# An attention and squared-ReLU kernel: its opening in a new load order, with most expanded weights spread by DMA, s applied at the eviction and the first attention put first

## The chip, the cores and the metric

The kernel runs on one core of one Trainium2 chip. The metric is the device time of a launch in microseconds (us). Engines: PE (TensorE), DVE (VectorE), ACT (ScalarE), POOL (GpSimd) and SP (SyncE), which here issues nearly all DMAs, in order.

## What is computed

```python
# x: (4, 12480, 128), inducing I: (32, 128), w_in: (128, 2048), w_out: (2048, 128); s, b: one number each
def mab(q, kv):
    a = softmax(q @ kv.T / sqrt(128))
    return a @ kv
h = mab(I, x)                     # 32 points for each of 4 batches
y = mab(x, h).reshape(49920, 128)
out = (s * relu(y @ w_in)**2 + b) @ w_out
```

## The kernel before

A block is 480 tokens (BLK), a tile two blocks (SB = 2); a batch has 13 tiles and 26 blocks. The last product is folded: y = A h, so y @ w_in is A times the small matrix h @ w_in. That matrix, 32 rows for a batch, is kept in `wst` as 128 rows: the rounded values twice and what rounding leaves twice ("expanded weights"). For each block the attention weights A, transposed and split in the same way, stand in a tile `a2t`. The steady work is 832 pairs (`pair(k)`, 8 pairs of 128 hidden columns x 2 in each of 104 blocks): two matmuls `wst` x `a2t` into `h` (L1002), a ReLU `r` (ACT or DVE), a rounded square (ACT, L1080), h times r (DVE, L1045), the difference to the rounded square (POOL or DVE, L1056), and six matmuls with `w_lo` and `w_hi` into the output bank (L1112). A block's output is evicted with a bias (L1125, L1127) and stored.

Which instruction comes when on each engine is decided at build time. `Plan` holds units of work (generators that yield an engine, a duration in us and events they wait for), gives each an urgency and always takes the one that its own clock has ready first, corrected by WEIGHT times urgency. `OPENING` is the set of constants for the first 16 pairs, the 26 sets of `STEADY` those for stretches of 32 pairs. Instructions stand in that order on each engine; on the chip semaphores enforce what depends on what.

The opening, in the order of its work:

- `opening()` issues the loads on SP. The tiles of batch 0 come in the order of `FIRST_GROUPS`; after the first the three small loads (inducing points `ind`, s, b) are issued, and after the places in `W_AFTER` one block of 512 columns of `w_in` or `w_out`. x tiles lie in five `xt` buffers, those in `X_HOME` in the buffers `gm` and `hm` of the later pairs.
- w_in and w_out come as 64-bit floats. `narrow` makes each block a 32-bit one with two maskings, two ACT steps, two DVE steps and a product on POOL or DVE; `split_w_out` multiplies a w_out block by s and splits it into `w_hi` (ACT, L455) and `w_lo` (DVE, L457).
- For each group `first_scores` makes the scores of the points, their exponentials and, with the tile not transposed, the values. The tile not transposed is made by `turn_x` (PE transposes L542, a copy for each half tile), or for those in `BY_DMA` loaded a second time as `xF` by `load_first`.
- When all maxima are there, `h_both` and `h_out` put the groups together and give `hT`, the 32 points.
- `w_unit` (four times) makes `wst` from `hT` and w_in: matmul L703, copy L705, subtraction L707. The later batches do it with `w_tiles` and `w_spread`: a matmul into 32 rows for each 512 columns, a copy and a subtraction into `whl`, and 16 DMA copies of 32 partitions into `wst`.
- `attend_first` makes `a2t` of block 0 alone, in a short form (L903 to L942). Then `front_work(0)` starts `attend(0, 0)` for blocks 1 to 3 (matmuls L853, a chain on DVE, copies L956 by DMA) and the bias. `keep_warm` puts matmuls on zeros into PE's gaps.

Of the kernel before, what the change touches and what calls it, by code (L numbers as in the profile page):

```python
# [56 lines left out]
W_IN_U = -100  # L57
W_OUT_U = -206.48
W_URGENCY = [12.71, 20.0, 50.1, 22.0]
W_LATE = -22.96  # L60
W_LEAN = {"Pool": -1.49}
FRONT_0 = -9.51
# [23 lines left out]
class Rules:  # L86
# [76 lines left out]
class Plan:  # L163
# [83 lines left out]
def tile_attn_relu2(ctx: ExitStack, tc: tile.TileContext, xT, xN, xF, indT, w_in, w_out, s_rep, b_rep, outT):  # L247
# [105 lines left out]
    def blocks_in(g):  # L353
        return min(GR, NBLK - g * GR)


    xt_tiles, xn_tiles = {}, {}
    raws = {}
    dma = [2.7]

    def landing(us):

        dma[0] = max(dma[0], plan.end + 3.0) + us
        if dma[0] < 5.0:
            dma[0], us = 6.2, dma[0]
            return us
# [962 lines left out]
```

## Time and profile before

| | |
|---|---|
| median of 3 runs | 1519.55 us (1518.22 to 1521.71) |
| the profiled execution: time / span | 1518.01 / 1516.2 us |
| busy: PE, DVE, ACT, POOL | 1495.3, 1435.3, 1465.4, 1443.7 us |
| granted TensorE clock, mean | 0.999 |
| first matmul of the first pair | 53.02 us |
| last matmul issued / last output DMA issued | near 1510.4 / 1511.96 us |

The span is from the first to the last thing that the profiler saw; the time of the execution is 1.8 us longer. A row gives the start or the window, then the busy time. PE's busy time overlaps from one matmul to the next, so that matmuls are better counted by their starts.

### The profile page before, as it was taken

What the parts mean: (1) busy time and instruction counts of PE and PEld (TensorE: products, weight loads), DVE (VectorE), ACT (ScalarE), POOL (GpSimd) and SP (SyncE); (2) the same over time, 40 slices, a digit from 0 to 9 for tenths busy, and PEclk for the clock granted to TensorE, in tenths of its full rate; (3) what the DMA queues carried; (4) which work ended last, traced back from release to release, by engine and by line L of the source; (5) the groups of instructions that cost most, each with busy time, mean ns of one, the idle gap of its engine ahead of it and who ended that gap; (6) DMA issues with size and microseconds to landing.
All of it is one profiled execution on the core that took longest, in us unless ns stands there. A gap on an engine that the chain in (4) does not pass through costs nothing.

```text
span 1516.2 us, 25236 instructions
## 1 busy us (share of the span) xinstructions
PE 1495.3 (99%) x8215; PEld 1294.9 (85%) x8215; DVE 1435.3 (95%) x1587; ACT 1465.4 (97%) x1767; POOL 1443.7 (95%) x725
## 2 busy tenths in 40 slices
PE   7899999999999999999999999999999999999998
PEld 5588888888888888888898888888889888888887
DVE  5899999999999999999999999999999999999998
ACT  6899999999999999999999999999999999999997
POOL 2599999999999999999999999999999999999998
PEclk9999999999999999999999999999999999999999
DMA  9244545534454454453455534544533334234332
GB/s 342 65 124 128 140 104 158 143 76 125 104 150 127 114 149 105 135 142 83 127 133 137 144 104 118 163 112 105 120 102 93 79 91 112 56 85 108 91 72 53
DMA packets 73810, 178.91 MB, mean 118 GB/s; under 512 B 13520, under 2 KB 40144, under 8 KB 73680
## 3 DMA queue, kind: packets, MB, share of 16 engines
q1 hardware_dynamic: 59280, 128.51, 27.2%
q0 software_dynamic: 14256, 48.67, 17.3%
q8 instruction: 67, 1.10, 0.3%
q14 instruction: 63, 0.52, 0.1%
q10 hardware_dynamic: 144, 0.12, 0.0%
HBM read 74.56 MB, written 25.56 MB: 66 GB/s over the span
## 4 chain that ended last, share of the span: by engine, by line
PE 69%; ACT 4%; issue 3%; POOL 3%; DVE 2%; DVEq 0%; ACTq 0%; POOLq 0%
PE x L1112 48%; PE h L1002 17%; POOL g L1056 3%; ACT r L1014 2%; ACT g L1080 2%; PE x L853 1%; DVE g L1045 1%; PE x L802 1%; PE x L762 1%; DVE h L1045 0%; DVE r L1016 0%; DVE gm L1027 0%; PE x L717 0%; ACT ob L1125 0%; POOL hm L1032 0%
## 5 line engine op out<-in xcount | busy, mean ns | idle before, releaser
L1056 POOL TENSOR_TENSOR g<-g,g 128x960 fp32r<-128x960 f32 x611 | 1399.2, 2665 | 21.7 <-DVE g L1045 13.4
L1112 PE MATMUL x<-g,w_hi 128*128 128x480 f32 x2932 | 920.1, 367 | 1.5 <-POOL g L1056 1.0
L1080 ACT ACTIVATE g<-r 128x960 fp32r<-128x960 f32 x733 | 713.4, 1008 | 12.0 <-PE x L1112 0.9
L1045 DVE SCALAR_TENSOR_TENSOR g<-h,r 128x960 f32<-128x960 f32 x611 | 688.5, 1146 | 24.2 <-ACT r L1014 13.7
L1014 ACT ACTIVATE r<-h 128x960 f32<-128x960 f32 x648 | 608.6, 970 | 12.5 <-PE h L1002 10.2
L1112 PEld LDWEIGHTS x<-g,w_hi 128*128 128x128 f32 x2932 | 550.8, 189 | 52.5 <-issue 6.3
L1112 PE MATMUL x<-g,w_lo 128*128 128x480 f32 x1466 | 537.4, 367 | 1.4 <-ACT g L1080 1.1
L1002 PE MATMUL h<-a2t,wst 128*128 128x480 f32 x1664 | 485.4, 374 | 3.7 <-DVE g L1045 3.2
L1002 PEld LDWEIGHTS h<-a2t,wst 128*128 128x128 f32 x1664 | 299.2, 189 | 82.2 <-issue 33.1
L1112 PEld LDWEIGHTS x<-g,w_lo 128*128 128x128 f32 x1466 | 277.0, 189 | 24.5 <-issue 2.6
L1016 DVE TENSOR_SCALAR r<-h 128x960 f32<-128x960 f32 x184 | 210.8, 1148 | 5.0 <-PE h L1002 3.8
L1056 DVE TENSOR_TENSOR g<-h,g 128x960 fp32r<-128x960 f32 x122 | 140.7, 1153 | 7.8 <-ACT g L1080 1.2
L1045 DVE SCALAR_TENSOR_TENSOR h<-h,r 128x960 f32<-128x960 f32 x122 | 141.0, 1155 | 0.9 <-ACT r L1014 0.8
L1027 DVE SCALAR_TENSOR_TENSOR gm<-h,r 128x960 f32<-128x960 f32 x99 | 113.3, 1145 | 4.3 <-ACT r L1014 4.1
L1032 POOL DMA_DIRECT2D hm<-gm x99 | 113.7, 1148 | 0.1
L1080 ACT ACTIVATE hm<-r 128x960 fp32r<-128x960 f32 x99 | 99.7, 1007 | 0.7
L1112 PE MATMUL x<-hm,w_lo 128*128 128x480 f32 x198 | 72.8, 368 | 0.0
L1112 PE MATMUL x<-hm,w_hi 128*128 128x480 f32 x198 | 72.5, 366 | 0.0
L1125 ACT ACTIVATE ob<-x,bias 128x480 f32<-128x480 f32 x101 | 66.8, 661 | 1.1 <-PE x L1112 0.5
L1112 PE MATMUL x<-hm,w_neg 128*128 128x480 f32 x198 | 56.3, 366 | 0.0
L1112 PEld LDWEIGHTS x<-hm,w_lo 128*128 128x128 f32 x198 | 37.4, 189 | 3.5 <-DVE hl L891 0.8
L1112 PEld LDWEIGHTS x<-hm,w_neg 128*128 128x128 f32 x198 | 37.4, 189 | 2.7
(152 smaller groups left out, 559.4 us busy)
## 6 DMA issues: line engine op xcount, KB each, us to landing
hm<-gm POOLq DMA_DIRECT2D x99, 480.0 KB, 5.3
xt<-in_xT_dram SPq DMA_DIRECT2D x96, 480.0 KB, 5.2
a2t<-hl SPq DMA_DIRECT2D x412, 60.0 KB, 2.0
out_dram<-ob SPq DMA_DIRECT2D x103, 240.0 KB, 2.1
xn<-in_xN_dram SPq DMA_DIRECT2D x18, 512.0 KB, 4.3
xn<-in_xN_dram SPq DMA_DIRECT2D x18, 448.0 KB, 4.8
wst<-whl SPq DMA_DIRECT2D x48, 64.0 KB, 2.0
g<-in_w_in_dram SPq DMA_DIRECT2D x4, 512.0 KB, 10.3
```

Of the source, the lines that this page charges most:

```text
L762: nc.tensor.matmul(ps[M * q:M * (q + 1), 0:BLK], ind_sb, xt[:, q % SB], start=True, stop=True)
L802: nc.tensor.matmul(ps[M * c:M * (c + 1), 0:P], eT[0:rows, n], xn_tiles[b, g, half][0][0:rows, n - half * TH], start=n < P // M, stop=n + P ...
L1002: nc.tensor.matmul(h[:, u, 0:BLK], wst[:, n * P:(n + 1) * P], by_turns(A), start=True, stop=True)
L1014: nc.scalar.activation(out=r, in_=hv, func=AF.Relu)
L1016: nc.vector.tensor_scalar(out=r, in0=hv, scalar1=0.0, scalar2=None, op0=ALU.max)
L1027: nc.vector.scalar_tensor_tensor(out=gm, in0=hv, scalar=-1.0, in1=r, op0=ALU.mult, op1=ALU.mult)
L1032: nc.gpsimd.dma_start(out=hi["t"].bitcast(F32).rearrange("p u t -> p (u t)"), in_=gm.rearrange("p u t -> p (u t)"), accum_op=ALU.add,)
L1045: nc.vector.scalar_tensor_tensor(out=g, in0=hv, scalar=0.0, in1=r, op0=ALU.max, op1=ALU.mult)
L1056: eng.tensor_tensor(out=g2, in0=g, in1=hi["t"].bitcast(F32), op=ALU.subtract)
L1080: nc.scalar.activation(out=hi["t"], in_=r, func=AF.Square)
L1112: nc.tensor.matmul(o, w, by_turns(g), start=first and n == 0, stop=left == 0 and n == len(ops) - 1)
L1125: nc.scalar.activation(out=ob, in_=o, func=AF.Identity, bias=bias, scale=1.0)
```

## The change

All of it is in the opening, except the eviction of each block, the last eviction, and the constants of `STEADY`.

- The loads follow a written list `ORDER`; i0 to i3 and o0 to o3 are blocks of w_in and w_out, f4 is the tile 4 loaded as `xF`. Four tiles come that way instead of two, into `g1` buffers instead of `xn`. `X_HOME` has three entries instead of six. The scores now wait for `ind`, which is ninth in the list.
- `FIRST_GROUPS` pairs other tiles; each weight block has an urgency of its own (`W_U`).
- `split_w_out` no longer multiplies by s: `w_hi` is a copy, `w_lo` a subtraction on DVE or POOL. The eviction multiplies by s instead.
- For batch 0 only the first 512 columns of `wst` come from `w_unit`; the other three quarters come from `w_tiles` and `w_spread`.
- `front_work(0)` waits until the second pair's matmuls are placed. `hold` keeps engines free for some time during `attend_first`.
- The last block is evicted in one piece by ACT and stored from ACT's queue.
- The planner's picture of the opening changes (engines begin at 0.7 to 2.3 us, PE takes twice as long before 8 us, an issue on SP takes 0.46 us), all constants of `OPENING` change, WEIGHT among them (0.0229 to 0.0032), and so do constants in most sets of `STEADY`.

```diff
-FIRST_GROUPS = ((2, 3), (4, 5), (6, 7), (8, 9), (10, 11), (12, 1), (0,))
-BY_DMA = [5, 9]
-W_AFTER = [1, 2, 6, 8, 1, 5, 7, 12]
-X_HOME = {3: "gm", 4: "hm", 5: "gm", 6: "hm", 8: "gm", 9: "hm"}
-FIRST_LEAN = {"ACT": -0.41}
+W_U = {"i0": 1513.8106, "i1": 2422.085, "i2": -276.0022, "i3": -391.7822, "o0": -749.0613, "o1": -185.0209, "o2": -164.7013, "o3": -106.3167}
+W_URGENCY = [-200.2675, 255.7455]
+FIRST_U = {"h": -16.5052, "sums": 121.8764, "attend": -87.9451}
+HOLD = [0.1554, 1.3641, 0, 0]
+W_LEAN = {"Pool": -1.9541}
+FIRST_GROUPS = ((2, 3), (4, 6), (5, 7), (8, 9), (12, 11), (10, 1), (0,))
+ORDER = [
+    "x2", "i0", "x3", "s", "x6", "x7", "x5", "i2", "ind", "f4", "x4", "i1", "x8", "x9", "x12",
+    "f11", "x11", "x10", "f9", "i3", "x1", "o0", "x0", "o1", "o3", "f1", "b", "o2",
+]
+ISSUE = 0.46
+BEGIN = {"SP": 0.74, "PE": 1.8, "ACT": 2.0, "DVE": 2.3, "Pool": 2.2}
+COLD = 8.0
+FIRST_LAND = 2.05
+X_HOME = {5: "hm", 6: "gm", 9: "hm"}
+FIRST_LEAN = {"ACT": -0.5563}
-OPENING = Rules(0.0229, 0.0865, -0.624, 0.022, ...)
+OPENING = Rules(0.0032, 0.1938, -0.1311, 0.0328, ...)
 STEADY = [
...
     def split_w_out(c):
...
-        nc.scalar.mul(w_hi[:, sl, :], raw[:, sl, :], s_sb)
-        yield "DVE", 0.63, LOCK
-        nc.vector.scalar_tensor_tensor(
-            out=w_lo[:, sl, :], in0=raw[:, sl, :], scalar=s_sb, in1=w_hi[:, sl, :].bitcast(F32),
-            op0=ALU.mult, op1=ALU.subtract,
+        nc.scalar.copy(out=w_hi[:, sl, :], in_=raw[:, sl, :])
+        yield dict(DVE=0.63, Pool=1.5), W_LEAN, LOCK
+        (nc.gpsimd if plan.eng == "Pool" else nc.vector).tensor_tensor(
+            out=w_lo[:, sl, :], in0=raw[:, sl, :], in1=w_hi[:, sl, :].bitcast(F32), op=ALU.subtract
         )
...
     def load_first(j):
-        n, free = ring_in_order("xn", 2)
+        yield "SP", ISSUE, room("g1", G1)
...
     def first_scores(g, ps, *waits):
...
-        yield "PE", 0.45 * len(js), *[("x", 0, j, 1) for j in js], *waits
+        yield "PE", 0.45 * len(js), "ind", *[("x", 0, j, 1) for j in js], *waits
...
     def w_tiles(b, ps, *waits):
-        yield "PE", 1.19, ("hT", b), *[("w_in", c) for c in range(F // WC)], *waits
+        yield "PE", 1.19, ("hT", b), *[("w_in", c) for c in range(F // WC)], *([] if b else [("wst", 0, 0)]), *waits
...
-        for c in range(F // WC):
+        for c in range(0 if b else 1, F // WC):
             plan.spawn(w_spread(b, c, whl, wst), SPREAD, plan.end + LAT)
...
     def attend_first():
...
+        hold(DVE=HOLD[0], Pool=HOLD[1])
...
         plan.set("first")
+        yield "SP", 0.0, ("mm1", 1)
         front_work(0)
...
     def out_part(k, ops, us, weights, used):
...
-        if blk_g == B * NBLK - 1:
-            for half, eng in ((0, "ACT"), (1, "DVE")):
-                plan.spawn(last_half(o, c0, half, eng), 0.0, plan.end + LAT)
-            return
-        yield dict(ACT=0.54, DVE=0.58), 0.0, "bias"
+        last = blk_g == B * NBLK - 1
+        yield dict(ACT=0.54) if last else dict(ACT=0.54, DVE=0.58), 0.0, "bias"
...
-            nc.scalar.activation(out=ob, in_=o, func=AF.Identity, bias=bias, scale=1.0)
+            nc.scalar.activation(out=ob, in_=o, func=AF.Identity, bias=bias, scale=s_sb)
...
-            nc.vector.tensor_scalar(out=ob, in0=o, scalar1=bias, scalar2=None, op0=ALU.add)
-        nc.sync.dma_start(out=outT[:, c0:c0 + BLK], in_=ob)
+            nc.vector.tensor_scalar(out=ob, in0=o, scalar1=s_sb, scalar2=bias, op0=ALU.mult, op1=ALU.add)
+        (nc.scalar if last else nc.sync).dma_start(out=outT[:, c0:c0 + BLK], in_=ob)
...
     def after():
...
-        for c in range(F // WC):
-            if c == F // WC - 1:
-                plan.spawn(with_spare(keep_warm), FIRST + 190.0)
-            plan.spawn(with_spare(w_unit, 0, c), FIRST + W_URGENCY[c])
-        plan.spawn(attend_first(), FIRST + 1.0)
+        plan.spawn(with_spare(w_unit, 0, 0), FIRST + W_URGENCY[0])
+        plan.spawn(with_spare(keep_warm), FIRST + 190.0)
+        plan.spawn(with_spare(w_tiles, 0), FIRST + W_URGENCY[1])
+        plan.spawn(attend_first(), FIRST + FIRST_U["attend"])
```

## Rows read from the trace of the kernel before

**Rows 1.** Windows: length; PE, PEld, DVE, ACT, POOL busy (x); clock; DMA share; GB/s

```profile
0.00:41.00 41.00, 32.89 (x422) 22.64 (x422) 20.71 (x51) 29.09 (x63) 8.54 (x12) 1.00 0.87 322
0.00:53.00 53.00, 43.94 (x494) 28.31 (x494) 30.38 (x76) 37.22 (x79) 11.08 (x14) 1.00 0.67 249
53.00:64.00 11.00, 7.53 (x36) 5.56 (x32) 10.83 (x16) 10.22 (x13) 5.97 (x4) 1.00 0.27 89
200.00:800.00 600.00, 599.61 (x3306) 524.70 (x3306) 577.15 (x631) 588.07 (x703) 588.55 (x293) 1.00 0.48 125
```

**Rows 2.** Waits of PE, 60 us to the end: total us, times, longest us

```profile
PE x L1112 <- POOL g L1056: 1.0, 2, 0.7
```

**Rows 3.** Windows of the load stream (columns as in rows 1)

```profile
0.00:30.00 30.00, 22.24 (x263) 14.96 (x263) 13.60 (x35) 19.20 (x39) 5.86 (x10) 1.00 0.93 347
5.00:10.00 5.00, 4.00 (x27) 2.34 (x25) 0.59 (x3) 1.76 (x3) 0.00 (x0) 1.00 0.98 350
15.00:20.00 5.00, 3.81 (x49) 2.13 (x45) 3.60 (x8) 3.85 (x10) 1.40 (x1) 1.00 1.02 417
```

**Rows 4.** DMA issues up to 40 us: count, KB each, median us to landing

```profile
xt<-in_xT_dram SPq DMA_DIRECT2D x10, 480.0 KB, 9.8
```

**Rows 5.** Timeline of SP's queue: start us, us, instruction

```profile
2.59 0.43 SPq L386 DMA_DIRECT2D gm<-in_xT_dram  x1
...
19.80 5.59 SPq L374 DMA_DIRECT2D xt<-in_xT_dram  x4
```

**Rows 6.** Timeline from the last tile's scores to hT

```profile
36.33 0.61 PE L568 MATMUL h<-xt,ind_sb 128*32 128x240 f32 x8
...
42.32 0.42 PE L603 MATMUL h<-r,eT 120*32 120x128 f32 x8 [0.32 <-ACT r L284]
...
45.24 0.29 DVE L690 COPY hT<-h 128x128 f32<-128x128 f32 x1 [0.85 <-PE h L687]
```

**Rows 7.** Timeline from hT to the first pair

```profile
47.02 0.30 DVE L909 TENSOR_TENSOR x<-x,mx 120x128 f32<-120x128 f32 x1
...
48.57 0.83 DVE L921 TENSOR_TENSOR s<-s,l 120x128 f32<-120x128 f32 x1
...
52.08 1.01 PE L853 MATMUL x<-xt,hT 128*32 128x480 f32 x8
...
53.02 1.48 PE L1002 MATMUL h<-a2t,wst 128*128 128x480 f32 x6
```

**Rows 8.** Timeline of the ramp: the fourth pair, two w_lo, the ninth pair

```profile
56.76 0.67 PE L1002 MATMUL h<-a2t,wst 128*128 128x480 f32 x2 [2.26 <-DVE g L1045]
...
60.71 1.25 DVE L457 SCALAR_TENSOR_TENSOR w_lo<-wst,s_sb,w_hi 128x512 fp32r<-128x512 f32 x1
...
70.24 0.67 PE L1002 MATMUL h<-a2t,wst 128*128 128x480 f32 x2
```

**Rows 9.** The tile a2t, 40 to 75 us: its copies by DMA

```profile
L956 SPq DMA_DIRECT2D a2t<-hl x12: 507/588/599, 63.4 to 70.5; - x12
...
DMA to landing us min/median/max: 1.9/2.0/2.0
```

**Rows 10.** Groups by line and shape up to 53 us: busy us, mean ns | idle before

```profile
L707 DVE TENSOR_TENSOR wst<-h,wst 64x512 fp32r<-64x512 f32 x4 | 2.7, 692 | 0.4 <-PE h L1258 0.2
...
L705 ACT CAST wst<-h 128x512 fp32r<-128x512 f32 x4 | 2.2, 586 | 0.8 <-PE h L703 0.7
```

**Rows 11.** Timeline near 30 us: DVE beside POOL

```profile
30.08 0.42 DVE L427 TENSOR_SCALAR g<-g 128x512 int32<-128x512 int32 x1
...
30.25 1.38 POOL L445 TENSOR_TENSOR w_in_sb<-w_in_sb,g 128x512 f32<-128x512 f32 x1 [0.74 <-DVE w_in_sb L442]
...
30.42 1.50 DVE L431 TENSOR_SCALAR g<-g 128x512 int32<-128x512 int32 x1
```

**Rows 12.** Timeline of the last evictions

```profile
1510.97 0.46 ACT L1095 ACTIVATE ob<-x,bias 128x240 f32<-128x240 f32 x1 [4.03 <-PE x L1112]
...
1511.46 0.47 DVE L1097 TENSOR_SCALAR ob<-x,bias 128x240 f32<-128x240 f32 x1 [2.07 <-ACT ob L1095]
```

More of the change, by code (lines that the diff above doesn't have):

```diff
@@ L238, in run @@
             idle = self.eng == "PE" and self.rules is not OPENING and at > self.free.get("PE", 0.0) + 1e-6
-            self.start, self.end = at, at + u[3][self.eng] + IDLE * idle
+            cold = self.eng == "PE" and at < COLD
+            self.start, self.end = at, at + u[3][self.eng] * (1 + cold) + IDLE * idle
             self.free[self.eng] = self.end
@@ L492, in tile_attn_relu2 @@
     home = {j: ("r", "xn")[n] for js in FIRST_GROUPS for n, j in enumerate(js)}
-    turned = [j for j in order if j not in BY_DMA]
+    by_dma = [int(n[1:]) for n in ORDER if n[0] == "f"]
+    turned = [j for j in order if j not in by_dma]
     def x_used(j):
@@ L505, in used @@
                 plan.set(("x", 0, j, 2))
[L507 removed]
+        left = [1 if j in by_dma else 2]
         return used
     def load_first(j):
[L511 to L514 removed]
+        yield "SP", ISSUE, room("g1", G1)
+        n = take("g1")
+        t = ew.tile([P, SB, NQ, P], F32, name="g1", bufs=G1)
         nc.sync.dma_start(out=t.rearrange("p a q c -> p (a q c)"), in_=xF[j])
[L516 removed]
+        xn_tiles[0, j] = [(t[0:T, a], ("g1", n)) for a in range(SB)]
         plan.events["xn", 0, j] = landing(1.3)
@@ L697, in w_unit @@
         sl = slice(c * WC, (c + 1) * WC)
-        yield "PE", 0.85, ("hT", b), ("w_in", c), *waits
-        if c == 0:
-            d["wst"] = wst_pool.tile([P, F], F32R, name="wst")
+        yield "PE", 0.94, ("hT", b), ("w_in", c), *waits
+        d["wst"] = wst_pool.tile([P, F], F32R, name="wst")
         wst = d["wst"]
@@ L895, in attend, with hold @@
             plan.spawn(spread(b, g, q), SPREAD, plan.end + LAT)
+    def hold(**engines):
+        for eng, us in engines.items():
+            plan.free[eng] = max(plan.free.get(eng, 0.0), plan.end + us)
     def attend_first():
-        yield "PE", 1.0, ("hT", 0), ("x", 0, 0, 2)
+        yield "PE", 0.93, ("hT", 0), ("x", 0, 0, 2)
         ps, hT = bank[1], st[0]["hT"]
@@ L922, in attend_first @@
         n, free = ring_in_order("hl", 2)
-        yield "ACT", 0.28, *free
+        hold(DVE=HOLD[2])
+        yield "ACT", 0.3, *free
         hl = p2.tile([P, 2, BLK], F32R, name="hl")
@@ L929, in attend_first @@
         nc.scalar.copy(out=hi, in_=both)
-        yield "DVE", 0.33
+        yield "DVE", 0.3
         nc.vector.tensor_tensor(out=lo, in0=both, in1=hi.bitcast(F32), op=ALU.subtract)
-        yield "PE", 0.3
+        hold(ACT=HOLD[3])
+        yield "PE", 0.4
         for q in range(NQ):
@@ L1088, in square @@
         )
-    def last_half(o, c0, half, eng):
-        yield eng, 0.33, "bias"
-        sl = slice(half * BLK // 2, (half + 1) * BLK // 2)
-        ob = p2.tile([P, BLK], F32, name="ob")
-        if eng == "ACT":
-            nc.scalar.activation(out=ob[:, sl], in_=o[:, sl], func=AF.Identity, bias=bias, scale=1.0)
-        else:
-            nc.vector.tensor_scalar(out=ob[:, sl], in0=o[:, sl], scalar1=bias, scalar2=None, op0=ALU.add)
-        issue = nc.scalar if eng == "ACT" else nc.sync
-        issue.dma_start(out=outT[:, c0 + sl.start:c0 + sl.stop], in_=ob[:, sl])
     def out_part(k, ops, us, weights, used):
@@ L1260, in keep_warm @@
     def keep_warm(ps, *waits):
-        while plan.events.get(("a2t", 0, 0), math.inf) > plan.end + 0.3:
+        for _ in range(40):
+            if plan.events.get(("a2t", 0, 0), math.inf) <= plan.end + 0.3:
+                break
             yield from warm(1, ps, *waits)
```

143 lines of the change are left out of this document (72 added, 71 removed).

## Prediction

> **What bounds the kernel now.** The page's totals come first: every engine is busy for 95 to 99% of the span, which says little, because it averages an opening and a body. The windows part them. From 200 to 800 us PE is busy for 599.6 of 600 us; up to 41 us it is busy for 32.9 of 41, DVE for 20.7, ACT for 29.1 [rows 1]. The list of PE's waits from 60 us to the end has five lines that add up to 3.8 us, the one shown among them [rows 2]. So after about 64 us the time is PE's own issue: 832 pairs with 8 matmuls each, 6,656 in all, at 0.2028 us from start to start (the planner's MM) are 1350 us, and the other batches' attention fills the rest. An edit that takes no matmul out of the body can gain there at most those 3.8 us and small gaps between starts. Before 64 us there are three stretches with limits of their own, and they are the case:
>
> 1. Loads. The ten x tiles in the xt buffers take 9.8 us (median) from issue to landing [rows 4], though one is 0.49 MB, 1.2 us of the stream of 417 GB/s that the window at 15 to 20 us shows [rows 3]: they queue behind each other. x0, the last tile, is issued at the end of the group of four at 19.80, about 25.4 us [rows 5], so it lands near 35.2; its scores start at 36.33 [rows 6].
> 2. From the last tile to hT. The last value matmuls start at 42.32, and hT is ready at 45.24 + 0.29 = 45.53 [rows 6].
> 3. From hT to the first pair, 53.02: 7.5 us of short dependent steps on PE, DVE and ACT [rows 7]. Behind it comes a ramp up to 64 us in which DVE (10.8 of 11 us) and ACT (10.2) are full and PE (7.5) is not [rows 1].
>
> What the change is worth is therefore: how much earlier does the first pair start, and is the ramp as long as before.
>
> **The change part by part.**
>
> *Load order.* In front of x0 the old order has 13 x tiles (480 KB), 4 w_in, 3 w_out and 2 xF tiles (512 KB): 10,848 KB. The new one has 13, 4, 1 and 3: 10,336 KB, so 512 KB less, 1.3 us. In the old order three small loads stand between x2 and x3 (x3 is issued at 2.59 us, three issues of 0.43 later than it could be [rows 5]) and the second 5 us run at 350 GB/s only, against 417 at 15 to 20 [rows 3]; the new order puts i0 there, ind ninth and b last but one. I take 1.4 us for that, bounds 0 and 2. But two more tiles come as xF, and f1, whose values the sixth group needs, stands three places behind x0. Up to f1 it is 12.16 MB. The window of the first 30 us gives 30 x 347 GB/s = 10.4 MB [rows 3]; the other 1.76 MB take 4.2 us at 417, and about 2 us pass from a transfer's start to its semaphore even when it is short (the a2t copies [rows 9]): 36.2 us on the old curve, 34.8 with 1.4 us gained. I take 35.3.
>
> *hT.* Behind f1 come half a group of value matmuls and what in the old trace runs from 42.32 to 45.53 [rows 6]: 3.2 us and 0.4 us for 16 matmuls in place of 8. hT at 38.9. A second bound is PE: it is busy 32.9 us up to 41 us [rows 1]; four half-tile transposes fewer, an estimate of 0.45 us each by the planner's own cost for them, leave 31, of which about 8 can be done before ind lands near 12 us (the scores wait for it now; it stands ninth, behind some 3.5 MB). 23 us from there at 95% end at 36, near the same moment. A third is x0's own chain: were it as slow as before (36.33 to 42.32, 6.0 us) it would end near 37.9 and hT at 41.1. I take 39.2, bounds 38.5 and 41.1: 6.3 us earlier (4.4 to 7.0).
>
> *hT to the first pair.* Putting attend(0, 0) behind the second pair takes its 0.94 us out of the way, 52.08 to 53.02 [rows 7]. It moves a whole unit: eight matmuls, a DVE chain of some 8 us, and 12 copies on SP for blocks 1 to 3. Block 1 has its first pair, the ninth, at 70.24 us [rows 8]; its four copies are issued by 65.8 and land near 67.8 [rows 9], so about 2.4 us of slack cover a start about 1 us later against the first pair. The hold on POOL during the softmax is worth 0.5 us: the divide L921 took 0.83 us beside a POOL multiply, while L909 of like size took 0.30 [rows 7]. Together 1.5 us, bounds 0.9 and 1.6. First pair: 45.53 - 6.3 = 39.2, and 7.5 - 1.5 = 6.0 behind it: 45.2 us, 7.8 us earlier.
>
> *Three quarters of the expanded weights by DMA.* Removed: three of the four L705 copies and L707 subtractions, at 0.59 and 0.69 us [rows 10], 1.8 us of ACT and 2.1 of DVE; added: one copy and one subtraction of like size, and 12 copies on SP. Nearest row: the a2t copies, 0.59 us issue each, 2.0 us to land [rows 9]. With whl ready some 4 us behind hT, block c1 is there at 43 + 2.4 + 2.0 = 47.4, c2 at 49.7, c3 at 52.1. Pair 2 needs c1: it comes 1.4 us after pair 1, where before it followed at once. In the old trace ACT gets to pair 2 late anyhow and pair 3 starts at 56.76, 3.7 us behind the first [rows 8], so this costs 0; without that cover it would cost 1.4. Behind these copies on SP stand only the a2t copies, some 10 us later.
>
> *s at the eviction, w_lo free to go to POOL.* The multiply by s leaves L455 and L457 and rides on an eviction that exists. A w_lo on DVE costs about 0.63 us of the pair's 1.25 [rows 8]; as a plain subtraction it may go to POOL, where the like multiply takes 1.38 [rows 11]. POOL is idle there, but DVE pays when the two meet: L431 took 1.50 us beside the POOL multiply at 30.25, against 0.42 for its neighbour L427 [rows 11]. Four such meetings are 4.3 us of DVE, none is a gain of 4 x 0.63 = 2.5; I take a gain of 1. The Trainium skill's page GPSIMD Engine Reference, Key points, speaks against this part: GpSimd shares its SBUF interfaces with VectorE and the latter is structurally about twice as fast at elementwise work. The trace agrees as far as 1.50 against 0.42 goes; by the page's rule alone the part would be a loss, some 4 us of DVE.
>
> *Ramp.* The opening loses 7.8 us on DVE and on ACT alike, 15.6 us of engine time. Work saved: four copies of 0.59 us, 2.5 us for the weights, 1 us for w_lo, about 6. The other 10 must come out of idle time; DVE was busy 30.4 and ACT 37.2 of the first 53 us [rows 1], so after their starts (near 9 and 5 us) some 23 us are there. Where they can't be used, w_out conversion falls into the ramp, as two w_lo (1.25 us at 60.71) do now [rows 8]. I take 0, bounds -2 and +3 (one w_out block more on DVE).
>
> *Tail.* One whole eviction on ACT in place of two halves in turn, 0.46 and 0.47 us [rows 12]: between nothing gained and the second half gone, 0.47; I take 0.2. *Body.* New priorities for 24 of 26 stages, no instruction added. Bounds: a gain of 3.8 us [rows 2]; a loss is open upward, see below. I take 0.
>
> **Sum.** 6.3 + 1.5 + 0 + 0.2 = 8.0 us. The profiled execution took 1518.0 us (span 1516.2): 1510.0. The median of the runs shown is 1519.55, 1.5 us above it, so the like median is 1511.5 us.
>
> **The rivals.**
>
> *A. Engine work sets the opening.* With loads 3 to 5 us earlier, the same chain of copies, exponentials and conversions on ACT binds; hT is at the third bound (41.1) and one w_out block falls into the ramp. For it: ACT was busy for 29.1 of the first 41 us and, once it had data, for nearly all of them [rows 1]. Against it: DVE may take the copies and was idle for 20 of these 41 us. Gain 4.4 + 1.5 + 0.2 - 2 = 4.1: 1515.4 us.
>
> *B. Ramp and body regain as well.* Conversions end ahead of the first pair, ramp 2 us shorter, half of the 3.8 us of waits goes: 3.9 us more, 1507.6 us.
>
> *C. The stream gets no denser.* X_HOME has three entries where it had six, so ten x tiles share five xt buffers, and SP, which issues in order, stands at a buffer that isn't free; the stream stays at the 350 GB/s of the second window [rows 3]. f1 then lands at 12.16 / 0.350 + 4.3 = 39.0 in place of 35.3: 3.7 us less, 1515.2 us. The Trainium skill's DMA: Bandwidth & Descriptors, Specifications, gives a limit of about 358 GB/s from HBM for one core, which would do the same; the row at 417 GB/s contradicts it here. This is also the case in which the change doesn't do what it says: a new order of loads that arrive no sooner.
>
> *D. Slower, by the body.* Priorities that suit the planner's durations but not the chip's put one PE wait more for a late POOL result into each of the 24 changed stages. A wait of this kind is 0.5 us (two, 1.0 us [rows 2]): 12 us, gain 8 lost: 1523.5 us. It decides the sign from 16 such waits on. For it: POOL is busy 588.6 of 600 us in the body [rows 1]. Against it: with rules of the same sort 832 pairs met these 3.8 us in all.
>
> **Chances.** Forecast 0.58, A 0.17, B 0.11, C 0.08, D 0.06. A measurement of this kernel can tell about 0.2% (3.0 us) from no change, so faster means below 1516.5 us. Forecast, B, 0.11 of A and 0.06 of C lie there: 0.86. The rest of A and C is no change, 0.08; D is 0.06 slower. The best ends of the terms give 7.0 + 1.6 + 2 + 0.5 + 2 = 13.1 (1506.4), the worst 4.4 + 0.9 - 3 = 2.3 (1517.2); the range 1506.0 to 1517.0 us holds A, B and C too, and leaves out D.
>
> **What would show it.** Right: first L1002 matmul near 45 us, f1's transfer as the last release ahead of h_out, attend(0, 0)'s matmuls behind two pairs, x0's scores near 32 us, the waits of PE behind 60 us still near 4 us. Wrong: SP waits for xt buffers between 10 and 25 us (C); a first pair near 48 and ACT full up to it (A); first pair near 45 but PE waits of 12 us behind it (D); w_out conversions of DVE between the first pair and pair 8 with pairs 3 to 7 further apart than now (ramp).

## The result, and the profile after

| | before | after |
|---|---|---|
| median of the runs compared (4 each) | 1518.88 us | 1531.16 us (1529.08 to 1534.93) |
| ratio after / before, 95% interval | | 1.0083 (1.0059 to 1.0107) |
| profiled execution: time / span | 1518.01 / 1516.2 us | 1532.97 / 1531.2 us |
| hT ready | 45.53 us | 44.66 us |
| start of the first pair (pair 0) | 53.02 us | 54.99 us |
| start of the ninth pair (pair 8) | 70.24 us | 72.12 us |
| start of the last pair (pair 831) | 1503.17 us | 1518.05 us |

The change makes the kernel 12.3 us slower; 8.0 us faster was forecast. Of the four executions, the two with a mean granted clock of 0.999 and 1.000 took 1529.1 and 1529.4 us, those with 0.993 and 0.995 took 1534.9 and 1533.0 (the profiled one), so some 4 to 6 us go along with the clock. By the starts of the pairs the 15.0 us between the two profiled spans fall into three parts: 1.9 us are lost up to pair 8, 13.0 us between pair 8 and pair 831 (1445.9 us where it was 1432.9), and 0.1 in the tail (13.14 against 13.05 us).

The windows of the profile after, with the columns and the stretches of [rows 1], and below them two shorter ones:

```profile
0.00:41.00 41.00, 33.32 (x426) 22.61 (x427) 18.06 (x50) 25.02 (x56) 7.83 (x12) 1.00 0.90 324
53.00:64.00 11.00, 9.45 (x35) 5.77 (x35) 8.76 (x14) 8.78 (x13) 7.26 (x5) 0.72 0.54 133
200.00:800.00 600.00, 599.04 (x3324) 522.44 (x3324) 578.39 (x633) 586.93 (x699) 593.54 (x296) 1.00 0.48 124
...
10.00:15.00 5.00, 2.12 (x18) 0.96 (x19) 0.23 (x1) 0.06 (x1) 0.00 (x0) 1.00 1.03 411
20.00:25.00 5.00, 5.00 (x84) 3.49 (x72) 3.25 (x7) 4.45 (x12) 0.14 (x1) 1.00 0.73 252
```

Between 10 and 15 us the DMA engines are full (411 GB/s), yet PE works for 2.1 us and ACT for 0.06: the data comes and nothing uses it. Between 20 and 25 us it is the other way round: PE is busy throughout, and the stream, which the prediction took to be dense, is at 252 GB/s. In the ramp the granted clock averages 0.72, so part of it ran at the lower level of 1.2 GHz; before it was 1.00 there.

Why PE stands still is in its waits up to 20 us (total us, times, longest us):

```profile
PE h L573 <- DMA ind_sb<-in_indT_dram: 4.0, 1, 4.0
```

The timeline has the first scores, and the tile `ind_sb` the time from issue to landing:

```profile
12.88 1.83 PE L573 MATMUL h<-xt,ind_sb 128*32 128x240 f32 x16 [3.97 <-DMA ind_sb<-in_indT_dram]
```

```profile
DMA to landing us min/median/max: 7.8/7.8/7.8
```

`ind`, 16 KB, is issued at 5.02 us as the ninth load and lands 7.8 us later, behind the tiles issued in front of it. The waits of SP's own queue up to 35 us show what follows: it stands for xt buffers that the late scores have not freed. (SP stood for the same readers before, 3.8 us for xt and 2.6 for `gm` and `hm` buffers; but there the stream is at 406 GB/s from 20 to 25 us.)

```profile
SPq L379 <- PE h L573: 8.4, 2, 5.8
```

From hT to the first pair (timeline; start, duration, instruction; the wait and its releaser in brackets; rows between are left out here):

```profile
44.38 0.28 DVE L695 COPY hT<-h 128x128 f32<-128x128 f32 x1
44.80 1.10 PE L707 MATMUL h<-w_in_sb,hT 128*128 128x512 f32 x2 [0.80 <-DVE hT L695]
46.49 0.65 PE L1269 MATMUL h<-hl 128*128 128x480 f32 x1
47.19 0.58 ACT L709 CAST wst<-h 128x512 fp32r<-128x512 f32 x1 [2.13 <-PE h L1269]
47.82 1.11 PE L1269 MATMUL h<-hl 128*128 128x480 f32 x2 [0.67 <-ACT wst L709]
49.04 0.69 DVE L711 TENSOR_TENSOR wst<-h,wst 64x512 fp32r<-64x512 f32 x1 [1.72 <-PE h L1269]
49.79 1.19 PE L1269 MATMUL h<-hl 128*128 128x480 f32 x2 [0.85 <-DVE wst L711]
54.99 1.91 PE L1020 MATMUL h<-a2t,wst 128*128 128x480 f32 x4
```

This takes 10.3 us where it took 7.5 [rows 7]. L1269 are the warming matmuls of `keep_warm`. ACT's copy of `w_unit` (L709) waits for a warming matmul, the next ones wait for that copy, DVE's subtraction (L711) waits for those, and the next for it: they take turns, and the DVE and ACT steps of `attend_first` are queued behind.

In the body, the waits of PE from 60 us to the end, which were 3.8 us in all [rows 2], are 10.5 us, with new lines at the head:

```profile
PE h L1020 <- DMA a2t<-hl: 4.1, 2, 2.5
PE h L1020 <- DVE g L1074: 1.8, 1, 1.8
...
PE x L1119 <- POOL g L1074: 0.6, 2, 0.3
```

At the first long wait the timelines of SP and of PE show:

```profile
109.25 0.34 SPq L1132 DMA_DIRECT2D out_dram<-ob  x1
109.64 2.42 SPq L974 DMA_DIRECT2D a2t<-hl  x4
...
116.45 0.64 PE L1020 MATMUL h<-a2t,wst 128*128 128x480 f32 x2 [2.54 <-DMA a2t<-hl]
```

The starts of PE's matmuls show three gaps of 2.9, 2.1 and 1.9 us (at 114, 1217 and 1438 us), each ahead of the first pair of a block whose `a2t` comes by copies; before had none of that kind.

### The profile page after: what moved, and what is told of

It reads as the page before. It is cut to its first block, busy times and chain, and to the rows that moved or that the text cites. A ratio compares the mean times of both kernels' runs of the same rounds, so it can differ in the third digit from the quotient of the medians.

```text
span 1531.2 us, 25252 instructions
## 1 busy us (share of the span) xinstructions
PE 1503.8 (98%) x8208; PEld 1297.9 (85%) x8208; DVE 1431.9 (94%) x1582; ACT 1464.9 (96%) x1755; POOL 1456.8 (95%) x733
## 3 DMA queue, kind: packets, MB, share of 16 engines
q1 hardware_dynamic: 60000, 130.22, 27.4%
## 4 chain that ended last, share of the span: by engine, by line
PE 78%; ACT 9%; issue 4%; DVE 4%; POOL 2%; DMA 2%; SPq 1%; ACTq 0%; DVEq 0%; POOLq 0%
PE x L1119 53%; PE h L1020 19%; ACT g L1098 4%; ACT r L1032 4%; DVE g L1063 1%; POOL g L1074 1%; PE x L859 1%; PE x L808 1%; PE x L768 1%; ACT hm L1098 1%; DMA a2t<-hl 1%; ACT ob L1129 1%; SPq L739 1%; DMA ind_sb<-in_indT_dram 1%; PE x L547 1%
## 5 line engine op out<-in xcount | busy, mean ns | idle before, releaser
L1034 DVE TENSOR_SCALAR r<-h 128x960 f32<-128x960 f32 x188 | 215.4, 1147 | 7.8 <-PE h L1020 6.1
L1074 DVE TENSOR_TENSOR g<-h,g 128x960 fp32r<-128x960 f32 x118 | 136.2, 1154 | 9.4 <-ACT g L1098 2.3
L1063 DVE SCALAR_TENSOR_TENSOR h<-h,r 128x960 f32<-128x960 f32 x118 | 136.4, 1156 | 1.6 <-ACT r L1032 1.4
L1129 ACT ACTIVATE ob<-x,bias,s_sb 128x480 f32<-128x480 f32 x101 | 76.1, 753 | 5.2 <-PE x L1119 5.0
```

Source lines behind the costliest of these rows:

```text
L1034: nc.vector.tensor_scalar(out=r, in0=hv, scalar1=0.0, scalar2=None, op0=ALU.max)
L1063: nc.vector.scalar_tensor_tensor(out=g, in0=hv, scalar=0.0, in1=r, op0=ALU.max, op1=ALU.mult)
L1074: eng.tensor_tensor(out=g2, in0=g, in1=hi["t"].bitcast(F32), op=ALU.subtract)
L1129: nc.scalar.activation(out=ob, in_=o, func=AF.Identity, bias=bias, scale=s_sb)
```

## The experiments

Theory 1: `ind`'s late landing holds up the opening and, since the order is fixed at build time, all behind it. Theory 2: the body's new order costs by itself. Theory 3: the lower clock behind hT is the loss. Times in the table are starts in each profiled execution; "body" is pair 8 to pair 831; the ratio is to the kernel before, run on the same chip.

| run | median us | ratio (95%) | hT ready | pair 0 | pair 8 | body |
|---|---|---|---|---|---|---|
| before | 1518.88 | | 45.53 | 53.02 | 70.24 | 1432.9 |
| after | 1531.16 | 1.0083 (1.0059 to 1.0107) | 44.66 | 54.99 | 72.12 | 1445.9 |
| e1_ind2 | 1528.76 | 1.0060 (1.0045 to 1.0075) | 40.77 | 50.64 | 67.47 | 1445.3 |
| e2_before_indlate | 1527.18 | 1.0050 (1.0033 to 1.0067) | 54.27 | 61.76 | 78.99 | 1433.6 |
| e3_warm2 | 1534.42 | 1.0094 (1.0079 to 1.0109) | 45.03 | 57.00 | 73.04 | 1446.9 |
| e4_ind2_warm2 | 1531.16 | 1.0076 (1.0061 to 1.0091) | 41.76 | 53.73 | 69.78 | 1447.2 |
| e5_ind2_outlate | 1521.66 | 1.0020 (1.0010 to 1.0029) | 40.89 | 50.85 | 67.59 | 1438.8 |
| e6_before_s | 1522.10 | 1.0024 (1.0014 to 1.0033) | 45.55 | 53.05 | 70.21 | 1436.4 |
| e7_ind2_oldrules | 1535.39 | 1.0107 (1.0090 to 1.0124) | 40.57 | 50.96 | 67.11 | 1454.9 |
| e8_s_in_weights | 1520.73 | 1.0009 (1.0000 to 1.0018) | 42.07 | 52.40 | 69.52 | 1437.0 |
| e9_warm_bank | 1518.53 | 0.9993 (0.9984 to 1.0001) | 41.39 | 48.19 | 65.40 | 1437.5 |
| e10_all | 1518.27 | 0.9998 (0.9989 to 1.0007) | 41.74 | 48.55 | 66.66 | 1437.1 |
| e11_after_warm_bank | 1529.59 | 1.0077 (1.0062 to 1.0093) | 45.88 | 52.62 | 69.72 | 1445.2 |
| e12_before_warm_bank | 1517.30 | 0.9993 (0.9985 to 1.0002) | 47.54 | 55.04 | 72.02 | 1433.2 |
| e13_before_sb_late | 1518.56 | 0.9997 (0.9988 to 1.0006) | 46.43 | 53.92 | 70.91 | 1433.0 |
| e14_four_units | 1536.90 (one) | | 41.41 | 48.81 | 66.96 | 1455.7 |
| e15_ind2_out_bank | 1518.75 | 1.0000 (0.9991 to 1.0010) | 40.80 | 47.54 | 64.63 | 1438.7 |

**ind early in the changed kernel, late in the one before.** In both, no compute engine's order changes.

```diff
-    "x2", "i0", "x3", "s", "x6", "x7", "x5", "i2", "ind", "f4", ...     # e1
+    "x2", "ind", "i0", "x3", "s", "x6", "x7", "x5", "i2", "f4", ...
...
+            if n == 3:                                                  # e2
+                nc.sync.dma_start(out=ind_sb, in_=indT)
             if n == 0:
-                nc.sync.dma_start(out=ind_sb, in_=indT)
                 nc.sync.dma_start(out=s_sb, in_=s_rep)
```

> The changed kernel with one load moved: ind is issued second, as in the kernel before, instead of ninth; the order of every other instruction on every engine is unchanged. Theory 1 (ind's late landing, 12.88 us where the written order counts on 2.6 us behind its issue, makes the whole opening run out of step): first scores near 8.5 us, full clock near 12, hT 40 to 41.5 instead of 44.7, first pair 47 to 50 instead of 55.2, no half clock behind hT, the three long waits for a2t copies in the body (2.9, 2.1, 1.9 us) gone or shorter; total 1516 to 1521 us. Theory 2 (the new priorities and order of the body are worse by themselves): the opening gains 3 to 5 us, but from pair 32 to pair 831 some 8 us are lost against the kernel before as they are now; total 1525 to 1528. Theory 3 (PE has too little to do behind hT, so that its clock falls): hT earlier, but the half clock behind it stays as long; total 1526 to 1529.

> The kernel before with one load moved: ind is issued behind three more loads (near 5 us instead of 1.2), every other instruction keeps its place. Theory 1: first scores near 11 to 12 us instead of 8.5, hT 2 to 3.5 us later than 45.5, total 1521 to 1526 us, 2 to 7 us slower than the kernel before. Theories 2 and 3: PE is not the bound of this opening, whose last tile lands near 35 us, so hT moves by less than 1 us and the total stays within 1.5 us of the kernel before.

In e1 `ind` lands 3.2 us after its issue, hT is ready 3.9 us earlier and pair 8 comes 4.65 us earlier. The opening moved as theory 1 said, if not quite as far: the first pair starts at 50.6 us where 47 to 50 was expected, and 3.4 us of lower clock are left behind hT. In e1 the stream stays dense and SP's wait for the readers is short (a window, and the same line of SP's waits as above):

```profile
20.00:25.00 5.00, 5.00 (x100) 3.61 (x95) 1.35 (x4) 4.23 (x12) 1.40 (x1) 1.00 1.02 407
```

```profile
SPq L379 <- PE h L573: 1.7, 2, 1.4
```

The body did not follow: 1445.3 us, as long as after's, and the total of 1528.8 is near what theory 2 expected. e2, the kernel before with `ind` late, in windows with the columns as above:

```profile
10.00:15.00 5.00, 0.00 (x0) 0.00 (x0) 0.52 (x3) 0.00 (x0) 0.00 (x0) 0.51 1.02 395
15.00:20.00 5.00, 3.58 (x24) 2.01 (x25) 1.82 (x5) 1.85 (x4) 0.00 (x0) 0.50 0.83 292
```

and its first scores in the timeline:

```profile
15.09 1.03 PE L568 MATMUL h<-xt,ind_sb 128*32 128x240 f32 x8 [6.83 <-DMA ind_sb<-in_indT_dram]
```

Issued three x tiles later, `ind` landed 9.6 us behind its issue. The first scores came 6.6 us later, hT 8.7, the end 8.1: more than the 2 to 7 us that I had expected. PE, idle for 6.8 us, then worked at the lower clock (0.51 and 0.50), which fits the difference but was not tested apart. So PE is the bound of this opening as soon as it starts late. The body kept its length to 0.7 us although all of it ran 8.7 us late: a late opening by itself does not put the body out of step, which takes the second half of theory 1 away.

**More warming matmuls.** A second one at each step of `keep_warm`, in after (e3) and in e1 (e4):

```diff
             yield from warm(1, ps, *waits)
+            nc.tensor.matmul(ps()[:, 0:BLK], warm_sb[:, 0:P], next(shapes), start=True, stop=True)
```

> The changed kernel with a second matmul of nothing at each step of keep_warm, the short loop that keeps PE busy while attend_first runs (two of 0.22 us where there was one); nothing else moves. Theory 3: the half clock between 49 and 59 us vanishes, and what follows hT runs at full clock: first pair 1 us earlier, pairs 2 to 8 about 2 to 4 us earlier; total 1523 to 1528. Theory 1: the clock returns, but the late start and the waits of the body stay: 1527 to 1530. Were the extra matmuls in the way of attend_first's own, first pair would be later by up to 1 us, total 1532.

> Both edits together. Theory 1: within 2 us of the run with ind second alone (1516 to 1521). Theory 3: 3 to 5 us below that run. Theory 2: not below 1522, since neither edit touches the body.

The windows of e3 behind hT:

```profile
41.00:53.00 12.00, 10.47 (x50) 6.08 (x50) 6.18 (x19) 5.83 (x13) 2.15 (x2) 1.00 0.21 81
53.00:64.00 11.00, 9.41 (x47) 5.51 (x46) 8.14 (x12) 8.30 (x12) 7.82 (x5) 1.00 0.42 109
```

The clock is 1.00 throughout, and the path from hT to pair 0 is 12.0 us instead of 10.3; the total is 3.3 us above after's median. e4 shows the same beside e1: 12.0 us in place of 9.9, and a total 2.4 us higher. Theory 3 falls: the lower clock accompanies the turn-taking, and more of what takes turns makes it longer.

**The body: SP's order, s, the priorities.** The gap at 109 us in e1, first the head of PE's waits behind 60 us:

```profile
PE h L1020 <- DMA a2t<-hl: 4.3, 2, 2.7
```

The timelines of SP's queue and of POOL:

```profile
104.61 0.34 SPq L1132 DMA_DIRECT2D out_dram<-ob  x1
105.00 2.43 SPq L974 DMA_DIRECT2D a2t<-hl  x4
...
106.20 0.89 POOL L1050 DMA_DIRECT2D hm<-gm  x1
```

The DMA queues from 108 to 110 us, of which there is this one (packets, MB, share of the 16 engines):

```profile
q0 software_dynamic: 106, 0.41, 118.7%
```

`hl`, from which the copies read, was ready at 103.8 us; SP stood at an output whose eviction ended only near 104.6. The last copy, issued at 106.8 behind POOL's 480 KB (issued at 106.2), took 5.0 us to land where the first took 1.9: from 108 to 110 us the DMA engines moved POOL's queue (q0) alone. The same output ahead of copies stands at the gaps near 1211 and 1432 us. e5 lets an output's transfer enter SP's order 3 us of planned time later:

```diff
-        (nc.scalar if last else nc.sync).dma_start(out=outT[:, c0:c0 + BLK], in_=ob)
+        if last:
+            nc.scalar.dma_start(out=outT[:, c0:c0 + BLK], in_=ob)
+        else:                        # out_late: yield "OUT", 0.0, then the same on nc.sync
+            plan.spawn(out_late(ob, c0), 0.0, plan.end + 3.0)
```

> ind second, and each output's transfer (out) put into SP's queue 3 us of planned time later, so that copies of a2t that become ready meanwhile stand ahead of it; the order on PE, ACT, DVE and POOL is unchanged. Theory 2a (of the 12.4 us that the body loses between pair 8 and pair 831, the larger part is three waits of PE for a2t copies, which stand on SP behind an out that waits for its eviction, and then meet the 480 KB transfer that POOL issues): the gaps at 109, 1211 and 1432 us (3.1, 2.2 and 1.9 us) shrink to under 0.5 us each, the body loses 5 to 7 us instead of 12.4, total 1521 to 1524 us. Theory 2b (the copies are late because the attention in front of them is late, whatever SP does): each gap loses at most 1 us, total 1526 to 1529.

The same place in SP's queue in e5:

```profile
103.21 2.47 SPq L974 DMA_DIRECT2D a2t<-hl  x4
```

and the head of PE's waits behind 60 us:

```profile
PE h L1020 <- DVE g L1063: 1.4, 5, 0.5
```

The copies start 1.8 us earlier, all three gaps are gone, no wait for `a2t` is left in the list, the body is 6.5 us shorter and the median 7.1 us lower (6.1 by the two ratios). Theory 2a holds. The Trainium skill (DMA: Bandwidth & Descriptors, Queues, rings and completion order) says that each DMA engine goes round robin between its queues, packet by packet. The trace of e1 does not show that here: SP's queue (q1) has no packet between 108 and 110 us while its copy is under way.

For s, the kernel before with `split_w_out` and the eviction of the change, and w_lo still on DVE:

```diff
-        nc.scalar.mul(w_hi[:, sl, :], raw[:, sl, :], s_sb)
+        nc.scalar.copy(out=w_hi[:, sl, :], in_=raw[:, sl, :])
...
-            nc.scalar.activation(out=ob, in_=o, func=AF.Identity, bias=bias, scale=1.0)
+            nc.scalar.activation(out=ob, in_=o, func=AF.Identity, bias=bias, scale=s_sb)
```

> The kernel before with one part of the change alone: s is applied at the eviction of the output, so that w_hi is a plain copy and w_lo a plain subtraction (on DVE as before); the order of all work is unchanged. If this part costs nothing, as the prediction has it: 1518 to 1520.5 us, pair 831 within 1 us of the kernel before. If the eviction with a scale from a tile, 0.75 us on ACT instead of 0.66, delays the body: up to 101 x 0.09 = 9 us, of which PE would see a part: 1521 to 1528 us.

The group of ACT's evictions in e6 (count, busy us, mean ns, idle before):

```profile
L1124 ACT ACTIVATE ob<-x,bias,s_sb 128x480 f32<-128x480 f32 x101 | 76.1, 753 | 0.8 <-PE x L1111 0.5
```

and the same group in the kernel before:

```profile
L1125 ACT ACTIVATE ob<-x,bias 128x480 f32<-128x480 f32 x101 | 66.8, 661 | 1.1 <-PE x L1112 0.5
```

An eviction with s takes 92 ns more, 9.3 us in all on ACT. Pair 8 does not move, and the body grows by 3.5 us, steadily; the median is 3.4 us higher. The Trainium skill (ScalarE: Activation LUTs, What ACT_TABLE_LOAD costs) gives about 93 ns for each operand that is a pointer to one value per partition; the trace agrees, with 92.

e7 gives e1 the body's constants (`STEADY`) of the kernel before:

> ind second, with the changed opening but the body's priorities of the kernel before; the order of the body comes out new, since it is worked out from both. By the written order's own times it should end 10.7 us later than with the new priorities. Theory 2 (the new priorities themselves are what costs in the body): the body from pair 8 on takes 1433 to 1437 us, as in the kernel before, and the total is 1516 to 1520. Rival (priorities suit only the opening they were fitted to; no set is good by itself): the body takes 1443 us or more, total 1526 to 1540.

The rival holds: with the old constants behind the new opening the body takes 1454.9 us, 22 us more than behind the old opening. These constants suit the plan that they were worked out for and not this one.

**All edits, and the shared tile.** e8 takes s out of the eviction without giving up the plain subtraction; e9 also sends the warming matmuls elsewhere. In both the term of b comes out times s, which the times don't feel; e10 adds the division (three small DVE steps and a reciprocal where there were two). e11, e12 and e15 have the second edit alone in other kernels.

```diff
+            nc.scalar.activation(out=dst, in_=m, func=AF.Identity, scale=s_parts[0], bias=s_sb)   # e8, w_out
-            nc.scalar.activation(out=dst, in_=m, func=AF.Copy, scale=2.0**-20, bias=1.0)
...
-            yield from warm(1, ps, *waits)                            # e9 to e12, e15, in keep_warm
+            yield from warm(1, lambda: bank[0], *waits)
```

> The run with ind second and late outs, with s taken out of the output's eviction again: here s goes into two steps that widen w_out's mantissa (scale and bias of the ACT step, scalar of the DVE step behind it), so that w_lo stays a plain subtraction that POOL may do; the order of all work is unchanged. If the eviction's scale costs in this body what it cost in the kernel before (3.4 us, growing along the 832 pairs): 1517.3 to 1519.3 us, pair 8 unmoved, the body 3 to 4 us shorter. Rival (ACT has slack in this body, so the longer eviction hides): 1520.5 to 1522.5.

> The same, and the warming matmuls of keep_warm write into bank 0, which is free then, where before they wrote into the other half of the tile that w_unit's copy and subtraction read. Theory (those three wait for each other through the shared tile: the subtraction of w_unit stood 1.7 us for a warming matmul, and DVE's next steps of attend_first behind it): the first pair comes 1.2 to 2.2 us earlier, near 49 to 50 us; of that 0.5 to 2 us reach the end: 1516 to 1518 us. Rival (ACT and DVE between 50 and 64 us are full, and take the gain back): first pair earlier, pair 8 and the total within 0.5 us of the run without this edit. Rival 2 (the wait has another cause): first pair within 0.3 us of 51.1.

> Ind second, late outs, s in w_out's widening, warming matmuls into bank 0, and b divided by s where the bias is made (in the two runs before this one the term of b came out times s; four small DVE steps are added). The time should be that of the run without the division: 1517.8 to 1519.3 us, first pair 48 to 49 us. Against the kernel before 0.9993 there, so no more than 1 us is left to win; if its opening (4.8 us earlier at pair 8) could keep all of it, 1515; the body of these priorities was longer by 4 to 4.5 us in the runs so far, and I expect that again.

> The changed kernel with one edit: the warming matmuls behind hT write into bank 0 instead of the tile's other half. ind stays ninth. Theory 4 (the 10.3 us from hT to the first pair, and the half clock behind hT, come from the warming matmuls that wait with w_unit through the shared tile): hT stays at 44.7, first pair 51.0 to 52.5 instead of 55.2, no half clock between 49 and 59 us; total 3 to 5 us shorter, 1525 to 1528. Theory 1 (they come from the late landing of ind, which puts all behind it out of step): first pair 54 to 55.2, total 1529 to 1531.

> The kernel before with the same edit to its keep_warm; the order of all work is unchanged. If the shared tile costs here too (the last of its four subtractions waits 0.2 us for a warming matmul, and four warming matmuls of 0.45 us stand among the short steps): first pair 0.3 to 1.2 us earlier, total 1518 to 1519. If not: 1519.3, within 0.5 us of the kernel before.

> Ind second, late outs and warm bank 0, with s at the eviction as in the changed kernel: the step between the run with late outs and the one with all edits. If the shared tile is worth here what the pair of runs with s in the weights showed (first pair 4.2 us earlier, 2.2 us of it at the end): first pair 47 to 49 us, total 1518.5 to 1520. If that gain belonged to chance in the clock: first pair 50 to 51, total 1521 to 1522.

e8 beside e5: the body is 1.9 us shorter, but pair 8 comes 1.9 us later, with 10.2 us of lower clock from 46.6 us on, and the median of 1520.7 lies in the rival's range, not in that of the theory. e9 beside e8: the first pair comes 4.2 us earlier, where 1.2 to 2.2 had been expected, and the median is 2.2 us lower.

e15 from hT to the first pair (line 1277 is the warming matmul here; rows between are left out):

```profile
40.52 0.28 DVE L695 COPY hT<-h 128x128 f32<-128x128 f32 x1
...
42.08 0.58 ACT L709 CAST wst<-h 128x512 fp32r<-128x512 f32 x1 [0.88 <-PE h L707]
42.64 2.27 PE L1277 MATMUL x<-hl 128*128 128x480 f32 x5
43.50 0.69 DVE L711 TENSOR_TENSOR wst<-h,wst 64x512 fp32r<-64x512 f32 x1
47.54 1.08 PE L1020 MATMUL h<-a2t,wst 128*128 128x480 f32 x4
```

In e15 the five warming matmuls run as one piece, L709 follows its own matmul, and hT to pair 0 takes 6.7 to 6.8 us (e9, e10, e11 and e15) against 9.9 to 10.4 without the edit. In e11 the clock is 1.00 from 41 to 64 us, with no more warming matmuls than after has. So the shared tile is the cause of the long path; that it also causes the lower clock fits e11 and e15, but e10 had another short stretch of it near 58 us. At the end, e5 to e15 gives 2.9 us. In e11 the median fell by 1.6 us only, within the two intervals, and to no less than after's own executions at full clock: the part of the shared tile in after itself is not separated from the clock. In the kernel before the edit changes nothing (7.50 us from hT to pair 0; ratio 0.9993, 1 within its interval): its four units stood in front of the warming.

The step from e15 to e10 (s out of the eviction) shortens the body by 1.6 us, from e15 to e9 by 1.2 and from e5 to e8 by 1.9, each in one profile; the medians of e15 and e10, 1518.75 and 1518.27, can't be told apart. In this body the eviction's 92 ns costs about half of the 3.5 us it costs in the old one.

**The small loads, and the spread by transfers.**

```diff
-                nc.sync.dma_start(out=s_sb, in_=s_rep)        # e13, in before: s at n == 4, b at n == 7
-                nc.sync.dma_start(out=b_sb, in_=b_rep)
...
-        plan.spawn(with_spare(w_tiles, 0), FIRST + W_URGENCY[1])     # e14
+        for c in range(1, 4):
+            plan.spawn(with_spare(w_unit, 0, c), FIRST + W_URGENCY[1])
```

> The kernel before with warming matmuls into bank 0 (as in the run before this batch) and the two small loads s and b issued three and six x tiles later; ind stays second, the order of PE, ACT, DVE and POOL is unchanged. If the small loads cost what the prediction took for them (1.4 us for three issues of 0.43 us in a stream that is limited by issues there, so 0.9 for two): x3 is issued 0.9 us earlier, the first scores and hT come 0.5 to 0.9 us earlier, total 0.5 to 0.9 us under the run without it, 1516.4 to 1517. Rival (the queue's depth hides issues, the bytes set the pace): hT within 0.2 us, total unchanged, 1517.3.

> Ind second, late outs, warm bank 0, and the four blocks of the expanded weights by four matmuls, copies and subtractions, as in the kernel before, instead of one block and three spread by transfers; the body's order changes with it (by the written order's own times its end is 18 us later), so only the times up to pair 8 count. If the spread by transfers costs nothing, as the prediction has it: first pair within 0.5 us of the run with the spread, pair 2 and pair 8 later by 1 to 3 us, as ACT and DVE get 1.8 and 2.1 us more to do. If it costs the wait that the prediction priced at 1.4 us without cover (pair 2 starts 4 us behind pair 1): pair 2 follows pair 1 within 2 us, and pair 8 is no later than with the spread.

e13: x3 is issued 0.94 us earlier, as expected, the total is not lower (1518.6 against 1517.3 in e12, both equal to before within their intervals); the hT of the two profiled executions can't be compared, as both hold stretches at the lower clock. Whether the issues cost anything stays open. e14: pair 2 follows pair 1 by 2.2 us instead of 4.0, but pair 1 comes 2.0 us behind pair 0 instead of 0.5, and pair 8 comes 2.3 us later than in e15, with one short stretch at the lower clock near 52 us in it. So far as this one run can tell, the spread is no worse than four units.

## Why the prediction was wrong

**Load order, predicted gain 6.3 us (hT), measured 0.9.** The step that failed is the second bound, PE, which was put at the same moment as the first and came out behind it. The late landing was seen ("near 12 us"; it was 12.88), but then it was reckoned that 8 of 31 us of PE's work could be done ahead of it. PE was busy for 5.9 us before 10 us, partly with warming, and did 12 of the transposes and no score; 27.4 of the 33.3 us up to 41 us (31 had been reckoned) came behind the landing, and the 3.2 us from the last values to hT belonged on top of this bound too, not only on the first. With `ind` early the term was 4.7 us (e15, hT at 40.80), inside its bounds of 4.4 to 7.0. The sum for the stream was right there: f1, forecast to land at 35.3 us, lands at 35.3 in e15 (38.6 in after), and what is missing of the 6.3 us lies behind it, 5.5 us from f1's landing to hT where 3.6 were taken. Rival C's sign was seen, SP's waits for xt buffers, though with another cause than fewer buffers: their readers were late, and with `ind` early the wait fell from 8.4 to 1.7 us (e1).

**hT to the first pair, predicted 6.0 us, measured 10.3.** That moving attend(0, 0) behind two pairs takes its 0.9 us out is right (L859 stands at 56.83). What was missed is a wait that the change adds: `w_unit` now stands among the warming matmuls and shares a tile with them. Without the sharing it is 6.7 us, 0.75 us better than before where 1.5 was predicted. The hold did what it was priced at: the divide (L936) takes 0.29 us in after, where it took 0.83 [rows 7].

**Spread of the weights, predicted 0.** Not contradicted: e14, a single run with a stretch at the lower clock, shows no gain without it. It started 10 us late (the first copies at 53.5 us, where whl was reckoned to be ready at 43), since hT and the path behind it were.

**s at the eviction, predicted as a gain of 1 us within the ramp.** This step failed in kind. I costed what leaves the opening, called the other side an eviction "that exists", and gave that nothing: 92 ns, 101 times, on an engine busy for 587 of 600 us. It costs 3.4 us alone (e6) and 1.2 to 1.9 in the body of the change.

**Ramp, predicted 0.** Right: from pair 0 to pair 8 it takes 17.1 us, before 17.2. It is 17.1 in e15 too, where the first pair starts 5.5 us earlier than before.

**Tail, predicted gain 0.2.** The last output's issue comes 8.6 us behind the start of the last pair instead of 8.8, but the end of the span 0.1 us later.

**Body, predicted 0, measured 13.0 us lost.** This is where the forecast went wrong most, and rival D, at 0.06, had its size (12 us) though not its mechanism: not small POOL waits in each stage, but three long ones for `a2t` copies. Of the 13.0 us, 6.5 are SP's order (e1 to e5) and 1.6 the eviction (e15 to e10); the body of after has six matmuls more than before between pair 8 and pair 831 (1.2 us at 0.2028), which before had done earlier; after's profile has a short stretch at the lower clock near 117 us, which e1's lacks, and its body is 0.6 us longer than e1's. The last two are reckoned, not tested. About 3 us are left that no run explains. I had argued that "rules of the same sort" met only 3.8 us of waits before; e7 and e14 show why that proves nothing: two other orders behind a new opening took 1454.9 and 1455.7 us.

**The range** of 1506 to 1517 left out just the case that came, because the body's loss was taken as "open upward" and then given no width.

No version is faster than the kernel before beyond its interval: e10 (0.9998) and e15 (1.0000) make up for all that the change lost and reach the kernel before; the gain of their opening, 3.6 and 5.6 us at pair 8, is spent in their body.

## What to carry to other kernels

When a schedule is written out ahead, check what each load's landing is assumed to be: a 16 KB load that everything waits for belongs in front, since behind 3.5 MB on the same queue it took 7.8 us and not the 2.6 that the plan allowed. An in-order queue should not hold something that nobody waits for (an output, standing for its eviction) ahead of something that the bound engine needs next. And an edit that "rides on" an instruction repeated a hundred times is costed by that instruction's own rows, not at nothing.

## What the runs showed of the hardware

In e1 a transfer that POOL issues (480 KB) had the 16 DMA engines to itself for 2 us, and a 60 KB copy of the other queue took 5.0 us to land instead of 1.9. PE's waiting costs twice in an opening: 6.6 us of later first scores in e2 became 8.7 us at hT, with the granted clock at 0.50 to 0.63 from 10 to 25 us. One more operand per partition on an ACT instruction of 480 columns costs 92 ns (e6 against before).
